# A fused linear-attention and max-out kernel on one core: the last scores of batch 0 moved between two projections, and four weight transposes moved into a wait

## The chip, the core and the metric

The kernel runs on one core of a Trainium2 chip. The core has TensorE (PE in the profile, with its weight loads as PEld), VectorE (DVE), ScalarE (ACT), GpSimd (POOL) and SyncE (SP), each with its own queue of instructions, worked off side by side and held together by semaphores; sixteen DMA engines move data between the chip's memory and the on-chip memory. Matmul results land in PSUM, which this kernel uses in banks of 128 x 512 numbers of 32 bits. The metric is the time of one execution on the device in microseconds (us), the median over runs.

## What is computed

Two stages, for 8 batches, 8 heads, 1024 positions and 64 features per head:

```python
k_proj = einsum('ks,bhsd->bhkd', E, k)          # 1024 positions -> 64
v_proj = einsum('ks,bhsd->bhkd', F, v)
scores = q @ k_proj.T / sqrt(64)
attn   = softmax(scores) @ v_proj               # 8 x 8 x 1024 x 64
x = attn.transpose(0, 2, 1, 3).reshape(8192, 512)
out = maximum(x @ w1, x @ w2) @ w_out           # 512 -> 1024 -> 512
```

## The kernel before

The kernel rewrites max(x w1, x w2) as relu(x (w1 - w2)) + x w2, so that out = relu(x wd) w_out + x m with wd = w1 - w2 and m = w2 w_out. For m it needs w2 transposed (`w2t_sb`); this takes 32 transposes of 128 x 128 on TensorE and copies out of PSUM on ScalarE. From batch 1 on, products are made with a seven-product (Strassen) scheme. Batch 0 is the start-up: its loads arrive piece by piece, and its order is written out by hand at L992 to L1041. The order of the program text is the order in every engine's queue, since scheduling is manual.

The steps that the change and the prediction speak of:

- `step_sc(t, g, j)` (L379): scores of head group g (four heads) and half j of the positions, 8 matmuls into a pair of "att" banks, then one exponential on ScalarE into `ex_sb`.
- `step_dn(t, g, j)` (L385): 8 matmuls with ones that sum the exponentials over the 64 projected positions, written over the scores' own bank pair, then a logarithm on ScalarE. `step_inv` (L428) turns it into the reciprocal (exponential of the negative) and sends a few rows by SyncE's queue to a table of checks.
- `step_kv(t, h0, h1, "v", ...)` (L185): projection of v for heads h0 to h1, 16 matmuls for two heads, then a cast to `vp_sb` by `copy` (DVE, or ACT for heads 4 to 8). `between` lets another step be issued between the two halves of its matmuls. v of batch 0 is loaded in four pieces of two heads.
- `step_at(t, g, j)` (L433): 16 value products (`values_into`, L365, through the helper at L355), into two "mm" banks or one att pair, then two multiplications by the reciprocal on DVE into `xt_sb`.
- `step_wd` (L543): w1 - w2 on DVE. `step_wd_rows` does the same in other pieces.
- `up_slots(t, j)` (L519): for half j the up blocks fb = 0 to 7 (called u0[fb] and u1[fb] after their half), each 4 matmuls of 128x512 into one mm bank, then a relu on ACT (DVE for fb = 3). The first two blocks of both halves are issued in two parts, `r1=2` and `r0=2`.
- `step_w2t(f0)` (L556): 8 transposes of w2 into one bank (an att bank with `att=True`), then one copy of 1024 on ACT.

PSUM is held in tiles by tag: four single banks mm0 to mm3 and two att pairs, used in turn. `mm_bank()` without a number takes the next of the list `turn`, which then moves on; with a number it takes that bank. An up block takes its bank by

```python
t["up", j, fb] = mm_bank(n=first_banks[j][fb] if r1 < NDC else fb % 2)
```

so the four blocks issued in two parts take their banks from `first_banks`, and later ones take bank 0 or 1. A bank can be written again when the last reader of its former tile is done. The order after L1041 is a list of slots: u0[0](r0=2), u0[1](r0=2), loads for batch 1, `step_w2t(256)`, u1[0](r0=2), u1[1](r0=2), subtractions, sums of x, u0[2], u0[3], then the Strassen products S1 and S2 (banks 2 and 3), the other transposes of w2, and so on.

Of the kernel before, what the change touches and what calls it, by code (L numbers as in the profile page):

```python
# [10 lines left out]
FP16 = mybir.dt.float16  # L11
# [8 lines left out]
def kernel(  # L20
# [12 lines left out]
    nc = tc.nc  # L33
# [29 lines left out]
    turn = [0, 1, 2, 3]  # L63

    def mm_bank(dtype=FP32, n=None):
        if n is None:
            n = turn.pop(0)
            turn.append(n)
        return ps.tile([128, 512 if dtype == FP32 else 1024], dtype, tag=f"mm{n}", name="mm_ps")

    def att_banks(dtype=FP32):
        return ps.tile(
            [128, 2, 512 if dtype == FP32 else 1024], dtype, tag="att", bufs=2, name="att_ps"
        )
# [4 lines left out]
    def big(n, dtype=FP16):  # L79
        return const.tile([128, 16384 // mybir.dt.size(dtype) // 2], dtype, tag=f"big{n}", name=f"big{n}")  # L80
# [45 lines left out]
    w2_sb = big(2).rearrange("p (r f) -> p r f", r=NDC)  # L126
    wo_sb = const.tile([128, NFB, DM], FP16, tag="wo", name="wo_sb")
    for g in range(2):
        for w_sb, w in ((w2_sb, moe_w2), (w1_sb, moe_w1)):
            nc.gpsimd.dma_start(  # L130
                out=w_sb.rearrange("p (g z) f -> p g z f", z=2)[:, g, :, 0:256],
                in_=w.rearrange("(g p z) f -> p g z f", p=128, z=2)[:, g, :, 0:256],
            )
    for w_sb, w, f0, f1 in (
# [3 lines left out]
        for z in range(2):  # L138
            nc.gpsimd.dma_start(
                out=w_sb.rearrange("p (g z) f -> p g z f", z=2)[:, :, z, f0:f1],  # L140
                in_=w.rearrange("(g p z) f -> p g z f", p=128, z=2)[:, :, z, f0:f1],
# [16 lines left out]
    ident16 = const.tile([128, 128], FP16)  # L158
# [26 lines left out]
    def step_kv(t, h0=0, h1=H, which="kv", att=False, dma=False, copy=nc.vector.tensor_copy, between=None):  # L185
        kv_ps = att_banks()[:, 0, :] if att else mm_bank(n=0 if dma else None)
        n = (h1 - h0) * D
        both = which == "v"
        nh = 2 if both else h1 - h0
        for h in range(0, h1 - h0, nh):  # L190
            if h and between is not None:
                between()
            for c in range(NC):
                for w in which:
                    i = "kv".index(w)
                    for r in range(2) if both else (i,):
                        nc.tensor.matmul(  # L197
                            out=kv_ps[r * KP : (r + 1) * KP, h * D : (h + nh) * D],
                            lhsT=eft[i][:, c, :],
                            rhs=t[w][:, h0 + h : h0 + h + nh, c, :],  # L200
                            start=(c == 0), stop=(c == NC - 1),
                        )
        zd = lambda ap: ap.rearrange("p (h d z) -> p h z d", d=D // 2, z=2)
        if "k" in which:
            eng = nc.vector.tensor_copy if which == "k" or dma else nc.scalar.copy
            kp = t["kp"][:, h0:h1]
            eng(out=kp[:, :, 0, :], in_=kv_ps[0:KP, 0:n].rearrange("p (h d) -> p h d", d=D))
        if both:
            copy(out=t["vp"][:, h0:h1], in_=zd(kv_ps[:, 0:n]))
        elif "v" in which:  # L210
            def finish_v():
                nc.vector.tensor_copy(out=t["vp"][KP:128, h0:h1], in_=zd(kv_ps[KP:128, 0:n]))
                if dma:
                    nc.vector.tensor_copy(out=kp[:, :, 1, :], in_=kp[:, :, 0, :])
                    step_kpt_dma(t)
                else:
                    step_vp(t, h0, h1)

            if att:
                return finish_v  # L220
            finish_v()


    def step_vp(t, h0=0, h1=H):
        fl = lambda ap: ap[:, h0:h1].rearrange("p h z d -> p (h z d)")
        nc.vector.tensor_copy(out=fl(t["vp"][0:KP]), in_=fl(t["vp"][KP:128]))
# [71 lines left out]
    def step_kpt_dma(t):  # L298
        nc.sync.dma_start_transpose(
            out=t["kpt"], in_=t["kp"].rearrange("p h r d -> p (h r d)")  # L300
        )
# [33 lines left out]
    def score(t, g, j, banks):  # L335
        for h in range(2):
            for o in range(2):
                for e in range(2):
                    head = 4 * g + 2 * h + e
                    z = D if t is tiles[0] else Z  # L340
                    for s in range(0, D, z):
                        pos = D * (o ^ e) + s
                        nc.tensor.matmul(  # L343
                            out=banks[e][pos : pos + z, h * W : (h + 1) * W],
                            lhsT=kpt_of(t, head, o)[:, s : s + z],
                            rhs=t["qt"][o * D : (o + 1) * D, head, j * W : (j + 1) * W],
                            start=True, stop=True,
                        )
        t["ex", g, j] = soft.tile([128, 2, HALF], FP16, tag="soft", name="ex_sb")
# [12 lines left out]
    def sums_into(t, g, j, dn_ps):  # L362
        tiles_into(lambda o: dn_ps[:, o, :], t["ex", g, j], lambda rows, hh: ones16[rows, 0:Z])
# [15 lines left out]
    def step_sc(t, g, j):  # L379
        sc_ps = att_banks()  # L380
        t["ps", g, j] = sc_ps
        score(t, g, j, [sc_ps[:, e, :] for e in range(2)])
        nc.scalar.activation(out=t["ex", g, j], in_=sc_ps, func=ACTF.Exp, scale=scale)

    def step_dn(t, g, j):  # L385
        dn_ps = t.pop(("ps", g, j))[:, :, 0:W]
        sums_into(t, g, j, dn_ps)
        ld = (ppool.tile([128, 2, W], FP32, tag="pd", bufs=4, name="ld_sb") if t is tiles[0]
              else soft.tile([128, 2, W], FP32, tag="soft", name="ld_sb"))
        t["ld", g, j] = ld  # L390
        nc.scalar.activation(out=t["ld", g, j], in_=dn_ps, func=ACTF.Ln)  # L391
# [4 lines left out]
    def check(inv):  # L396
        rows = checked[4 * n_checked[0] : 4 * n_checked[0] + 4, :]
        n_checked[0] += 1
        nc.sync.dma_start(
            out=rows, in_=inv.rearrange("(a z) o w -> a z (o w)", z=Z)[:, 0, :]  # L400
        )
# [26 lines left out]
    def step_inv(t, g, j):  # L428
        ld = t["ld", g, j]
        nc.scalar.activation(out=ld, in_=ld, func=ACTF.Exp, scale=-1.0)  # L430
        check(ld)
# [84 lines left out]
    w2t_sb = big(3).rearrange("p (f m) -> p f m", f=NFB)  # L516
# [32 lines left out]
    def step_wd_rows(f0):  # L549
        for z in range(2):  # L550
# [2 lines left out]
                out=rows(wd_sb), in0=rows(w1_sb), in1=rows(w2_sb), op=ALU.subtract  # L553
            )

    def step_w2t(f0, att=False, hold=False):  # L556
        ps_t = att_banks(FP16)[:, 0, :] if att else mm_bank(FP16)
        for f in range(2):
            for r in range(NDC):
                nc.tensor.transpose(  # L560
                    out=ps_t[:, (f * NDC + r) * 128 : (f * NDC + r + 1) * 128],
                    in_=w2_sb[:, r, f0 + f * 128 : f0 + (f + 1) * 128],
                    identity=ident16,
                )
        fb = f0 // 128

        def copy():
            nc.scalar.copy(
                out=w2t_sb[:, fb : fb + 2, :].rearrange("q f m -> q (f m)"), in_=ps_t
            )  # L570

        if hold:
            box["w2t"] = copy
        else:
            copy()
# [9 lines left out]
    CH = DM // 2  # L585
# [406 lines left out]
    t = tiles[0]  # L992
# [26 lines left out]
    warm(2)  # L1019
    step_sc(t, 1, 0)  # L1020
    step_kv(t, 0, 2, "v")
    step_kv(t, 2, 4, "v")
    step_dn(t, 1, 0)
    step_sc(t, 1, 1)
    step_at(t, 0, 0)
    step_at(t, 0, 1)
    step_inv(t, 1, 0)
    step_kv(t, 4, 8, "v", True, copy=nc.scalar.copy, between=lambda: step_dn(t, 1, 1))
    step_inv(t, 1, 1)
    att_banks()  # L1030
    for f0 in (0, 128):
        step_wd(f0, 0, 2, 128)
# [1 line left out]
    u0, u1 = [*up_slots(t, 0)], [*up_slots(t, 1)]  # L1034
    step_wd(0, 2, 4)
    step_at(t, 1, 1, True)
    first_banks = turn[0:2], turn[2:4]
    for i in range(2):
        for u in u0, u1:
            u[i](r1=2)  # L1040
    step_w2t(0, True)  # L1041


    load_all(tiles[1], 1, "k", k)
    wt = [lambda f0=f0: step_w2t(f0) for f0 in range(0, DF, 256)]
    wd = [lambda f0=f0: step_wd_rows(f0) for f0 in range(0, DF, 256)]
    f = lambda s, *a: lambda: s(tiles[0], *a)

    def loads(b, *names):
# [19 lines left out]
    slots = [  # L1069
        lambda: u0[0](r0=2), lambda: u0[1](r0=2), lambda: loads(1, "v", "q", "k"),  # L1070
        lambda: step_w2t(256, True),
        lambda: u1[0](r0=2), lambda: u1[1](r0=2), wd[1], lambda: sums_x(U[0, 1], range(4)),
        u0[2], u0[3], S1, S2, lambda: step_w2t(512, True), lambda: step_w2t(768, True, True), wd[2],
# [41 lines left out]
    t = tiles[1]  # L1115
    for n, x in enumerate((
# [4 lines left out]
        for name in x.split():  # L1121
# [6 lines left out]
            else:  # L1128
                g, j = int(name[2]), int(name[3])
# [14 lines left out]
    t = tiles[2]  # L1144
# [8 lines left out]
    for b in range(3, B):  # L1153
        t = tiles[b]
# [25 lines left out]
    for n, (b, o) in enumerate(units):  # L1180
# [14 lines left out]
        if n:  # L1195
            end = ("U", n - 1, 1, 6) if n > 1 else ("P", 0, 6, 1)
            m = 0 if n == last else 2
# [17 lines left out]
    for key, slot in slots:  # L1215
        r = slot()
        pending = [g for g in [r, *(f() for f in pending)] if g is not None]
        for s in steps.pop(key, ()):
            r = s()
# [5 lines left out]
    for reg in regs:  # L1225
# [4 lines left out]
        out=mm_bank()[0:1, 0:1], lhsT=ones16[:, 0:1], rhs=ones16[:, 0:1], start=True, stop=True  # L1230
# [166 lines left out]
```

## Time and profile before

| | us |
|---|---|
| median of three runs | 319.62 (319.59 to 319.87) |
| the profiled execution | 319.29 |
| its span, first to last instruction | 317.5 |

The span is the time that the profile shows; the 1.8 us around it are start and end of the execution. The mean granted TensorE clock of the execution is 0.999 of full speed.

How to read the rows. A row of the timeline has start and duration in us, the engine, the line of the kernel, the operation, the tile written and the tiles read, partitions x elements and type, and the count of instructions merged into the row; in brackets stands the idle time of the engine before it and what ended that. Matmuls overlap, so that a row of them can reach past the start of the next; the distance between starts is what they cost. A row of waits has the total, the number of waits and the longest. A row of a stretch has its limits, its length, then busy time and count for PE, PEld, DVE, ACT and POOL, the granted clock, the DMA share and GB/s.

### The profile page before, as it was taken

To read this page: it belongs to the slowest core of one execution; us is meant where nothing else is said; L and a number is where in the kernel's file an instruction comes from. 1 tells how busy PE (TensorE), PEld (TensorE's weight loads), DVE (VectorE), ACT (ScalarE), POOL (GpSimd) and SP (SyncE) were. 2 spreads that over 40 slices of the span, in tenths; PEclk is the share of its full clock that TensorE was granted. 3 is DMA by queue.
4 is the path that set the end of the run, shared out by engine and by line. 5 is a ranking of instruction groups with operands and counts; after the bars stand their busy time and mean duration, and the time that the engine had idled before them with its cause. 6 is when DMAs were issued, how large, how long until landed. Compare 5 with 4: busy or idle time off the path is not lost.

```text
span 317.5 us, 9309 instructions
## 1 busy us (share of the span) xinstructions
PE 311.7 (98%) x3902; PEld 254.9 (80%) x3902; DVE 244.9 (77%) x474; ACT 206.9 (65%) x375; POOL 39.7 (13%) x63
## 2 busy tenths in 40 slices
PE   7989999999999999999999999999999999999996
PEld 3656688788887888788887888788887888888885
DVE  3368997977969696996969696996969696969883
ACT  2477843767776777477776777476776777765541
POOL 8269002011000400003000300003000000000000
PEclk9999999999999999999999999999999999999999
DMA  8999999999978799997999699987998431313134
GB/s 190 206 201 199 207 206 202 208 166 165 185 144 193 135 195 245 235 190 118 226 242 243 124 199 246 218 164 124 224 222 204 90 101 36 103 34 102 35 102 136
DMA packets 76685, 53.72 MB, mean 169 GB/s; under 512 B 29664, under 2 KB 76128, under 8 KB 76640
## 3 DMA queue, kind: packets, MB, share of 16 engines
q0 software_dynamic: 30688, 28.05, 56.2%
q1 hardware_dynamic: 45664, 24.85, 31.5%
q8 instruction: 31, 0.51, 0.7%
q10 hardware_dynamic: 288, 0.20, 0.2%
q14 instruction: 14, 0.11, 0.1%
HBM read 57.15 MB, written 16.78 MB: 233 GB/s over the span
## 4 chain that ended last, share of the span: by engine, by line
PE 92%; DMA 5%; POOL 1%; ACT 1%; issue 0%; DVE 0%; POOLq 0%
PE mm_ps L874 47%; PE mm_ps L766 28%; DMA v_sb<-in_v_dram 4%; PE att_ps L355 3%; PE mm_ps L528 3%; PE mm_ps L197 3%; PE mm_ps L343 2%; PE att_ps L239 1%; PE att_ps L644 1%; PE mm_ps L644 1%; DMA out_dram<-o_sb 1%; PE mm_ps L313 1%; PE att_ps L560 1%; POOL k_sb L108 0%; POOL q_sb L108 0%; ACT ld_sb L391 0%
## 5 line engine op out<-in xcount | busy, mean ns | idle before, releaser
L736 ACT COPY p_sb<-mm_ps 128x512 f32<-128x512 f32 x180 | 102.4, 592 | 47.3 <-PE mm_ps L766 27.2
L874 PEld LDWEIGHTS <-big 128*128 128x128 f16 x768 | 73.5, 98 | 11.8 <-issue 3.6
L874 PE MATMUL mm_ps<-T_sb,big 128*128 128x256 f16 x576 | 76.9, 273 | 0.0
L781 DVE TENSOR_TENSOR gt_sb<-mm_ps,p_sb 128x512 f16<-128x512 f32 x58 | 39.9, 688 | 42.8 <-PE mm_ps L766 41.4
L766 PE MATMUL mm_ps<-big,big 128*128 128x256 f16 x348 | 52.2, 273 | 0.0
L766 PEld LDWEIGHTS <-big 128*128 128x128 f16 x464 | 45.4, 98 | 5.9 <-DVE big L607 0.2
L874 PE MATMUL mm_ps<-wo_sb,gt_sb 128*128 128x256 f16 x256 | 42.6, 273 | 0.0
L874 PEld LDWEIGHTS <-gt_sb 128*128 128x128 f16 x376 | 35.7, 98 | 6.7 <-issue 2.7
L472 ACT ACTIVATE ex_sb<-mm_ps 128x512 f16<-128x512 f32 x50 | 27.2, 596 | 18.0 <-PE mm_ps L343 12.3
L766 PEld LDWEIGHTS <-wd_sb 128*128 128x128 f16 x348 | 34.1, 98 | 4.4
L766 PE MATMUL mm_ps<-xt_sb,wd_sb 128*128 128x256 f16 x232 | 33.8, 273 | 0.0
L502 DVE TENSOR_TENSOR xt_sb<-att_ps,ld_sb 128x1024 f16<-128x1024 f32 x26 | 31.7, 1218 | 0.2
L874 PE MATMUL mm_ps<-m_sb,xt_sb 128*128 128x256 f16 x128 | 24.5, 273 | 0.0
L905 DVE TENSOR_TENSOR o_sb<-mm_ps,p_sb 128x512 f32<-128x512 f32 x32 | 21.8, 683 | 2.8 <-ACT p_sb L934 2.0
L784 DVE TENSOR_SCALAR gt_sb<-gt_sb 128x512 f16<-128x512 f16 (+1 forms) x62 | 21.8, 351 | 2.1
L305 POOL COPY junk<-qt_sb 1x1 f16<-1x1 f16 x6 | 1.4, 238 | 174.1 <-DMA qt_sb<-q_sb 174.1
L719 DVE TENSOR_TENSOR big<-gt_sb 128x1024 f16<-128x1024 f16 x32 | 21.8, 682 | 0.0
L874 PE MATMUL mm_ps<-wo_sb,big 128*128 128x256 f16 x128 | 21.5, 273 | 0.0
L843 ACT ACTIVATE gt_sb<-mm_ps 128x512 f16<-128x512 f32 x29 | 17.4, 600 | 5.9 <-PE mm_ps L766 5.9
L874 PE MATMUL mm_ps<-T_sb,gt_sb 128*128 128x256 f16 x120 | 20.3, 273 | 0.0
L781 DVE TENSOR_TENSOR gt_sb<-p_sb 128x512 f16<-128x512 f32 x29 | 19.8, 682 | 0.6 <-ACT p_sb L736 0.6
L874 PEld LDWEIGHTS <-xt_sb 128*128 128x128 f16 x188 | 18.3, 98 | 2.3 <-issue 0.2
(123 smaller groups left out, 432.9 us busy)
## 6 DMA issues: line engine op xcount, KB each, us to landing
out_dram<-o_sb SPq DMA_DIRECT2D x62, 256.0 KB
k_sb<-in_k_dram POOLq DMA_DIRECT2D x7, 1024.0 KB, 10.2
v_sb<-in_v_dram POOLq DMA_DIRECT2D x7, 1024.0 KB, 17.0
q_sb<-in_q_dram POOLq DMA_DIRECT2D x5, 1024.0 KB, 23.5
q_sb<-in_q_dram POOLq DMA_DIRECT2D x6, 512.0 KB, 16.1
big<-in_moe_w_dram POOLq DMA_DIRECT2D x12, 128.0 KB, 6.5
v_sb<-in_v_dram POOLq DMA_DIRECT2D x4, 256.0 KB, 13.4
wo_sb<-in_moe_w_out_dram POOLq DMA_DIRECT2D x1, 1024.0 KB, 10.3
```

What stands on the lines that cost most here:

```text
L197: nc.tensor.matmul(out=kv_ps[r * KP : (r + 1) * KP, h * D : (h + nh) * D], lhsT=eft[i][:, c, :], rhs=t[w][:, h0 + h : h0 + h + nh, c, :], ...
L355: nc.tensor.matmul(out=dst(r ^ (hh % 2))[hh * Z : (hh + 1) * Z, :], lhsT=weights(rows, hh), rhs=ex[rows, hh % 2, hh // 2 * W : (hh // 2 + ...
L472: nc.scalar.activation(out=t["ex", g, j][:, e, :], in_=banks[e], func=ACTF.Exp, scale=scale)
L502: nc.vector.tensor_tensor(out=x_out(t, g, j).rearrange("q z o n -> q o z n"), in0=at_ps.rearrange("q o (z n) -> q o z n", z=2), in1=ld[:, ...
L719: nc.vector.tensor_tensor(out=S(i), in0=S(0) if x is None else x, in1=y(), op=op)
L736: copy(out=x, in_=bank)
L766: nc.tensor.matmul(out=bank[:, m * W : (m + 1) * W], lhsT=w_[:, n_, (2 * d + m) * 128 : (2 * d + m + 1) * 128], rhs=a[:, n_, :], start=(n ...
L781: nc.vector.tensor_tensor(out=c_blk(j, c), in0=two(x), in1=two(y), op=ALU.add)
L784: nc.vector.tensor_scalar_max(ap, ap, 0.0)
L843: nc.scalar.activation(out=out, in_=in_, func=ACTF.Relu)
L874: nc.tensor.matmul(out=bank[i][:, 0:CH] if two_banks else bank[:, i * CH : (i + 1) * CH], lhsT=a(c)[:, i * 128 : (i + 1) * 128], rhs=w_(c) ...
L905: nc.vector.tensor_tensor(out=o_sb, in0=two(x), in1=two(y), op=ALU.add)
```

## The change

In the hand-written order of batch 0, sc(1,1) goes ahead of the second v projection; dn(1,1) goes ahead of the projection of heads 4 to 8, which is issued in one piece; four of the first eight transposes of w2 (the row blocks r = 0 and 1 of the first two column blocks) go behind that projection into a single mm bank, with their copy behind the second reciprocal; the other four stay where all eight were. The bank used is the first of `turn`, which is not moved on, and the banks of the first up blocks are shifted by one, so that the last of them, u1[1], gets the bank of the four transposes.

```diff
+    def step_w2t_half(g, ps_t):
+        for f in range(2):
+            for z in range(2):
+                r = 2 * g + z
+                nc.tensor.transpose(
+                    out=ps_t[:, (f * 2 + z) * 128 : (f * 2 + z + 1) * 128],
+                    in_=w2_sb[:, r, f * 128 : (f + 1) * 128], identity=ident16,
+                )
+        return lambda: nc.scalar.copy(
+            out=w2t_sb[:, 0:2, g * CH : (g + 1) * CH],
+            in_=ps_t[:, 0 : 2 * CH].rearrange("q (f m) -> q f m", f=2),
+        )
+
     step_sc(t, 1, 0)
     step_kv(t, 0, 2, "v")
+    step_sc(t, 1, 1)
     step_kv(t, 2, 4, "v")
     step_dn(t, 1, 0)
-    step_sc(t, 1, 1)
     step_at(t, 0, 0)
     step_at(t, 0, 1)
     step_inv(t, 1, 0)
-    step_kv(t, 4, 8, "v", True, copy=nc.scalar.copy, between=lambda: step_dn(t, 1, 1))
+    step_dn(t, 1, 1)
+    step_kv(t, 4, 8, "v", True, copy=nc.scalar.copy)
+    w2t_copy = step_w2t_half(0, mm_bank(FP16, turn[0]))
     step_inv(t, 1, 1)
+    w2t_copy()
     att_banks()
...
-    first_banks = turn[0:2], turn[2:4]
+    first_banks = turn[1:3], (turn[3], turn[0])
     for i in range(2):
         for u in u0, u1:
             u[i](r1=2)
-    step_w2t(0, True)
+    step_w2t_half(1, att_banks(FP16)[:, 0, :])()
```

## The prediction

> **What bounds the kernel now.** I read the page first, then the list of what TensorE (PE) waited for, then the timeline from 17 to 30 us, where the edited steps lie.
>
> ```profile
> PE 311.7 (98%) x3902; PEld 254.9 (80%) x3902; DVE 244.9 (77%) x474; ACT 206.9 (65%) x375; POOL 39.7 (13%) x63
> ...
> PE 92%; DMA 5%; POOL 1%; ACT 1%; issue 0%; DVE 0%; POOLq 0%
> ```
>
> ```profile
> ...
> PE mm_ps L1229 <- DMA out_dram<-o_sb: 1.2, 1, 1.2
> PE att_ps L355 <- ACT vp_sb L209: 0.5, 1, 0.5
> PE mm_ps L197 <- DMA v_sb<-in_v_dram: 0.4, 1, 0.4
> PE att_ps L355 <- ACT ex_sb L383: 0.2, 1, 0.2
> ```
>
> The page's two rows are busy time by engine and the chain that ended last by engine. The four rows of PE's waits (total, times, longest) are all of its waits from 17 us to the end. The L1229 wait is the very last instruction. So from 22.6 us to about 313 us PE never stands still, and whatever PE gains or loses before about 30 us moves the end by the same amount: there is no later wait that could give back a gain or swallow a loss. The three short waits, 1.1 us together, are what the change can go for.
>
> ```profile
> 17.68 0.64 PE L197 MATMUL mm_ps<-v_sb,eft 128*64 128x128 f16 x16
> 18.77 0.64 PE L197 MATMUL mm_ps<-v_sb,eft 128*64 128x128 f16 x16 [0.45 <-DMA v_sb<-in_v_dram]
> 19.34 0.30 PE L355 MATMUL att_ps<-ex_sb,ones 64*32 64x256 f16 x8
> 19.57 0.41 PE L343 MATMUL att_ps<-qt_sb,kpt_sb 64*64 64x256 f16 x8
> 19.91 0.63 PE L355 MATMUL mm_ps<-ex_sb,vp_sb 64*32 64x256 f16 x32
> 20.47 0.64 PE L197 MATMUL att_ps<-v_sb,eft 128*64 128x128 f16 x16
> 21.27 0.30 PE L355 MATMUL att_ps<-ex_sb,ones 64*32 64x256 f16 x8 [0.16 <-ACT ex_sb L383]
> 21.50 0.64 PE L197 MATMUL att_ps<-v_sb,eft 128*64 128x128 f16 x16
> 22.61 0.63 PE L355 MATMUL att_ps<-ex_sb,vp_sb 64*32 64x256 f16 x32 [0.47 <-ACT vp_sb L209]
> 23.21 1.90 PE L528 MATMUL mm_ps<-xt_sb,wd_sb 128*128 128x512 f16 x8
> 24.95 0.61 PE L560 MATMUL att_ps<-ident,big 128*128 128x128 f16 x8
> 25.39 1.03 PE L528 MATMUL mm_ps<-xt_sb,wd_sb 128*128 128x512 f16 x4
> 26.26 0.61 PE L560 MATMUL att_ps<-ident,big 128*128 128x128 f16 x8
> 26.70 2.75 PE L528 MATMUL mm_ps<-xt_sb,wd_sb 128*128 128x512 f16 x12
> 29.29 0.49 PE L766 MATMUL mm_ps<-xt_sb,wd_sb 128*128 128x256 f16 x3
> ```
>
> These are start and duration. A row's price on PE is the distance to the next start, since matmuls overlap: 16 of a v projection 0.57 (18.77 to 19.34), 8 sums 0.23, 8 scores 0.34, 32 value products 0.56, 8 transposes 0.44 (so four 0.22), four 128x512 matmuls 0.87. The twelve at 26.70 are the second halves of up blocks u1[0] and u1[1], then u0[2] and u0[3]; 2.59/12 = 0.216 each puts u0[2] at 26.70 + 4 x 0.216 = 27.56. That moment is my yardstick.
>
> **The change part by part.**
>
> *The last scores, sc(1,1), ahead of the second v projection.* They run from 18.25 (17.68 + 0.57) to 18.59, inside the DMA wait that ends at 18.77, and cost nothing there; with that cover gone they would cost 0.34. What they leave behind is not worth 0.34 either, for the next value products wait for a cast:
>
> ```profile
> 19.45 0.29 DVE L209 CAST vp_sb<-mm_ps 128x128 f16<-128x128 f32 x1 [0.79 <-PE mm_ps L197]
> 20.47 2.48 DVE L446 TENSOR_TENSOR xt_sb<-mm_ps,ld_sb 128x512 f16<-128x512 f32 x4 [0.73 <-PE mm_ps L355]
> 22.87 0.48 DVE L544 TENSOR_TENSOR wd_sb<-big,big 128x256 f16<-128x256 f16 x2
> ...
> 24.80 1.28 DVE L446 TENSOR_TENSOR xt_sb<-att_ps,ld_sb 128x512 f16<-128x512 f32 x2
> ```
>
> ```profile
> 17.81 1.02 ACT L383 ACTIVATE ex_sb<-att_ps 128x1024 f16<-128x1024 f32 x1 [0.55 <-PE att_ps L343]
> 19.71 0.60 ACT L391 ACTIVATE ld_sb<-att_ps 128x512 f32<-128x512 f32 x1 [0.88 <-PE att_ps L355]
> 20.20 1.02 ACT L383 ACTIVATE ex_sb<-att_ps 128x1024 f16<-128x1024 f32 x1
> ...
> 22.18 0.37 ACT L209 CAST vp_sb<-att_ps 128x256 f16<-128x256 f32 x1
> 22.45 0.63 ACT L430 ACTIVATE ld_sb<-ld_sb 128x512 f32<-128x512 f32 x1
> ```
>
> The vector engine's (DVE's) cast ends at 19.74; a hop to PE is 0.06 (ACT's cast ends at 22.55, PE goes on at 22.61). So at(0,0) starts at 19.80 in place of 19.91: gain 0.11, with bounds 0 and 0.34. On ScalarE (ACT) the exponential of sc(1,1) moves from 20.20 to about 18.8, into idle time, and the logarithm at 19.71 stays.
>
> *dn(1,1) ahead of the last v projection, which is no longer split.* Value products 19.80 to 20.36, dn(1,1) to 20.59 without its 0.16 wait (the exponential is done at 19.8), first half of the projection to 21.16. The second half needs the last piece of v:
>
> ```profile
> L108 POOL DMA_DIRECT2D v_sb<-in_v_dram x2: 738/746/755, 6.3 to 7.0; - x2
> DMA to landing us min/median/max: 13.7/14.0/14.3
> ```
>
> These are the last two v issues; the later one, at 7.0, lands at 7.0 + 14.3 = 21.3. So a stall of 0.18 comes in the middle, the second half starts at 21.34 where it started at 21.50, and the rest follows 0.16 earlier: ACT's cast 22.02 to 22.39, at(1,0) at 22.45. No DMA issue changes its place in SyncE's or GpSimd's queue.
>
> *Four transposes in the wait for that cast.* PE is free from 21.91 to 22.45 and they take 0.22: free. Their bank, number 0, is left by DVE's first product at about 21. If the wait were gone they would cost the 0.22 that the shorter block at 24.95 saves. Their copy follows the reciprocal on ACT, 22.83 to about 23.4, before u1[1] first writes the bank at about 24.4.
>
> *Up to here.* DVE's products run back to back from 20.47, so they too come only 0.11 earlier, and the up blocks, which wait for the subtraction at 22.87, start at 23.10. Eight matmuls to 24.84, four transposes to 25.06, u0[0] and u0[1] to 25.93. The eight transposes of the next block need the bank that DVE leaves at 26.08 - 0.11 = 25.97, so 26.03 to 26.47, and u1[0], u1[1] to 27.34. That is a gain of 0.22, and it would be the whole story were the banks as before.
>
> *The banks of the up blocks.* After 24 turns the list stands at 0, 1, 2, 3. Before, u0[0], u0[1], u1[0], u1[1] got 0, 1, 2, 3; now they get 1, 2, 3, 0. The next block, u0[2], has bank fb % 2 = 0 fixed in the code. It therefore used to wait for the relu of u0[0], the oldest; it now waits for the relu of u1[1], the block computed immediately before it. In the changed kernel's order this shows: u0[2]'s first matmul waits for ACT and the three blocks after it need no further wait.
>
> ```profile
> 25.59 1.01 ACT L568 COPY big<-att_ps 128x1024 f16<-128x1024 f16 x1 [2.51 <-PE att_ps L560]
> 26.50 1.09 ACT L537 ACTIVATE gt_sb<-mm_ps 128x512 f16<-128x512 f32 x2
> 27.47 1.03 ACT L568 COPY big<-att_ps 128x1024 f16<-128x1024 f16 x1
> 28.36 1.62 ACT L537 ACTIVATE gt_sb<-mm_ps 128x512 f16<-128x512 f32 x3
> ```
>
> ACT's order is copy, two relus (u0[0], u0[1]), copy, two relus (u1[0], u1[1]). From start to start a big copy takes 0.90, a relu 0.49 ((27.47 - 26.50)/2). Before, u1[1]'s relu began at 28.85, but only the second Strassen product at 29.7 needed it. Now: the half copy is not in the trace; it lies between the cast of 256 (0.37) and the copy of 1024 (1.01), and I take the relu's 0.49, of 512 elements from the same memory. It starts 0.42 after its transposes (24.95 to 25.59 is 0.64, less 0.22), at 25.26; relus at 25.75 and 26.24; the big copy at 26.73 (its transposes are ready at 26.03 + 0.64 = 26.67); u1[0]'s relu at 27.62, u1[1]'s at 28.11, done at 28.71 with 0.60; u0[2] at 28.76.
>
> PE has nothing else to do from 27.34 to 28.76: behind u0[2] in its queue stand u0[3] and all later products, and ACT's relu of u0[2] and DVE's of u0[3] wait for these. The stall is 1.42 and the sum 1.42 - 0.22 = **+1.20 us**. Bounds: no gain at the value products gives +1.31; DVE as early as PE's own work allows (up blocks at 23.01) +1.11; a half copy as dear as the big one, +1.61; free, +1.15 (the relus then follow PE).
>
> The Trainium skill, "PSUM — Partial Sum Buffer", section "Engine vs sequencer instructions", says that ScalarE's queue is strictly first in, first out. By that rule u1[1]'s relu can't pass the big copy, and the sum stays at +1.20. Were it wrong, the relu could start with u1[1]'s end, and the sum would be that of the third case below.
>
> **The rivals.** (a) *The bank does not bind*, and only the gain stays: 319.62 - 0.22 = 319.4. u1[1]'s relu would have to end by 27.28, and ACT's rows put it 1.4 later; for it speaks only that ACT may take the half copies faster than any row here, or the bank order may be other than I read. This is the other side: not slower.
>
> (b) *The clock falls in the stall.* The first matmuls of the kernel ran at half the later speed, and PE's clock stayed full over a shorter wait:
>
> ```profile
> 1.47 3.60 PE L153 MATMUL mm_ps<-ones 128*128 128x512 f16 x8 [1.47 <-DVE ones L146]
> ```
>
> ```profile
> 21.50:22.61 1.11, 0.64 (x25) 0.48 (x17) 1.11 (x3) 1.11 (x4) 1.07 (x2) 1.00 1.44 192
> ```
>
> Eight 128x512 matmuls took 3.60 there against 8 x 0.216 = 1.73 now. If the stall brought that state back for u0[2] and u0[3], eight such matmuls, 1.8 us would come on top: 322.6. Against it: in the second row PE was busy for 0.64 of 1.11 us and the last-but-two number, the clock, stayed 1.00. The Trainium skill, "TensorE: Matmul & The Clock Gate", section "What's actually happening", has the clock halve after an idle window of about 3.4 us; a stall of 1.42 is shorter, and no run here shows that window.
>
> (c) *ACT frees the bank without the big copy ahead of it*: relu of u1[1] behind that of u1[0] from 27.1, done near 28.2, +0.6 to +0.7: 320.3. Against it stands that the rows at 26.50, 27.47 and 28.36 run in program order.
>
> (d) *The loss is absorbed later*, 319.6 to 320.2. The list of waits leaves no place for it.
>
> **How the numbers follow.** The profiled execution took 319.29 us (span 317.5 and 1.8 around it); with +1.20 it would be 320.49. The median of the runs is 0.33 higher, so the forecast for the median is 319.62 + 1.20 = 320.8. Chances: forecast 0.80, (a) 0.07, (b) 0.04, (c) 0.06, (d) 0.03. Less than 0.2%, or 0.64 us, can't be told from no change. The forecast is slower by 0.38%, and its bounds of +1.11 to +1.61 all are; (a) is mostly within, (c) on the edge, (d) within. So slower 0.83, the same 0.13, faster 0.04. The range from 320.2 to 321.5 takes in the bounds, the scatter of 0.3 among the runs before, and (c).
>
> **What would show it.** In the changed profile PE's waits should list a new one, L528 on ACT's relu, of about 1.4 us, near 27.3; it should end with the second relu after the big copy. sc(1,1) should lie at about 18.3, at(0,0) at 19.8, the up blocks at 23.1, u0[2] near 28.8, and everything after it 1.2 us later with no other new wait. Of PE's old waits for the exponential and for v's second piece the first should be gone and the second shortened. I am wrong if u0[2] follows u1[1] directly, or if a wait after 30 us shrinks by what this one costs.

## The result, and the profile after

The changed kernel takes 320.89 us (median of 18 runs, 320.53 to 323.14) against 319.71 us (18 runs, 319.36 to 320.48) beside it: 1.18 us more, ratio 1.0038 with a 95% interval of 1.0029 to 1.0046. It is slower, by the amount that was forecast. Its profiled execution took 320.90 us with a span of 319.0. The ratios, here and below, leave out slow executions, of which there is one, 1126.80 us among the nine of experiment e4 (its median keeps it), and they need not equal the quotient of the two medians.

PE's waits in the changed kernel (total, times, longest):

```profile
PE mm_ps L153 <- DVE ones L146: 1.5, 1, 1.5
PE mm_ps L528 <- ACT gt_sb L537: 1.2, 1, 1.2
PE mm_ps L1245 <- DMA out_dram<-o_sb: 1.2, 1, 1.2
PE att_ps L197 <- DMA v_sb<-in_v_dram: 0.2, 1, 0.2
PE att_ps L343 <- DVE qt_sb L318: 0.2, 1, 0.2
PE mm_ps L197 <- DMA v_sb<-in_v_dram: 0.2, 1, 0.2
```

The three waits that the change went for are smaller or gone: the one for ACT's cast of v (0.5) and the one for the exponential (0.2) are no longer listed, the one for v's second piece fell from 0.4 to 0.2. In their place stands a wait of an up block (L528) for a relu (L537), larger than all three together, and v's last piece is now waited for. PE's timeline around it, start and duration first:

```profile
17.59 0.41 PE L343 MATMUL att_ps<-qt_sb,kpt_sb 64*64 64x256 f16 x8
...
18.50 0.41 PE L343 MATMUL att_ps<-qt_sb,kpt_sb 64*64 64x256 f16 x8
19.07 0.64 PE L197 MATMUL mm_ps<-v_sb,eft 128*64 128x128 f16 x16 [0.16 <-DMA v_sb<-in_v_dram]
...
21.64 0.64 PE L197 MATMUL att_ps<-v_sb,eft 128*64 128x128 f16 x16 [0.24 <-DMA v_sb<-in_v_dram]
22.29 0.40 PE L560 MATMUL mm_ps<-ident,big 128*128 128x128 f16 x4
22.73 0.63 PE L355 MATMUL att_ps<-ex_sb,vp_sb 64*32 64x256 f16 x32
23.38 1.90 PE L528 MATMUL mm_ps<-xt_sb,wd_sb 128*128 128x512 f16 x8
25.11 0.39 PE L560 MATMUL att_ps<-ident,big 128*128 128x128 f16 x4
25.34 1.03 PE L528 MATMUL mm_ps<-xt_sb,wd_sb 128*128 128x512 f16 x4
26.40 0.61 PE L573 MATMUL att_ps<-ident,big 128*128 128x128 f16 x8
26.84 1.03 PE L528 MATMUL mm_ps<-xt_sb,wd_sb 128*128 128x512 f16 x4
29.09 1.89 PE L528 MATMUL mm_ps<-xt_sb,wd_sb 128*128 128x512 f16 x8 [1.23 <-ACT gt_sb L537]
30.82 1.04 PE L779 MATMUL mm_ps<-xt_sb,wd_sb 128*128 128x256 f16 x8
```

In the kernel before, twelve matmuls stood in one row from 26.70: u1[0], u1[1], u0[2], u0[3]. Now the row is broken after four. Counted from start to start, u1's four cost 4 x 0.216 = 0.86 from 26.84, so PE stood from 27.70 to 29.09, 1.39 us. (The row's 1.23 counts from the modelled end of the last matmul.) The chain of waits of the same execution says what it waited on, link by link:

```profile
25.28 0.24 PE att_ps L560 x4
25.52 0.02 issue
25.54 0.58 ACT big L564
26.12 0.99 ACT gt_sb L537 x2
27.11 0.94 ACT big L581
28.05 1.00 ACT gt_sb L537 x2
29.05 0.04 issue
29.09 1.89 PE mm_ps L528 x8
```

Half copy, two relus, big copy, two relus, and 0.04 later u0[2]: for 3.5 us the time of the kernel is set by ACT.

The two profiled executions did not start alike: v's first projection, ahead of which nothing was changed, began at 17.68 before and at 17.93 here. The second, which follows the landing of its piece of v in both, began at 18.77 and at 19.07. So I compare by the distance from that start to u0[2]: 27.56 - 18.77 = 8.79 before, 29.09 - 19.07 = 10.02 here, +1.23. The rest of the 1.53 by which u0[2] is later here is the later start. What becomes of it afterwards is in the chain's last links, of the kernel before and of the changed one:

```profile
313.59 1.98 DMA out_dram<-o_sb
```

```profile
315.12 1.98 DMA out_dram<-o_sb
```

The last store starts 1.53 later, exactly as u0[2] does: over 285 us nothing was given back and nothing was added.

### The profile page after: what moved, and what is told of

It reads as the page before. It is cut to its first block, busy times and chain, and to the rows that moved or that the text cites. A ratio compares the mean times of both kernels' runs of the same rounds, so it can differ in the third digit from the quotient of the medians.

```text
span 319.0 us, 9309 instructions
## 1 busy us (share of the span) xinstructions
PE 312.7 (98%) x3902; PEld 254.9 (80%) x3902; DVE 244.7 (77%) x474; ACT 207.2 (65%) x376; POOL 39.9 (13%) x63
## 4 chain that ended last, share of the span: by engine, by line
PE 91%; DMA 5%; POOL 2%; ACT 1%; issue 0%; DVE 0%; POOLq 0%
PE mm_ps L887 47%; PE mm_ps L779 28%; DMA v_sb<-in_v_dram 5%; PE att_ps L355 3%; PE mm_ps L197 3%; PE mm_ps L528 3%; PE mm_ps L343 2%; PE att_ps L239 1%; PE att_ps L657 1%; PE mm_ps L657 1%; POOL v_sb L108 1%; ACT gt_sb L537 1%; DMA out_dram<-o_sb 1%; PE mm_ps L313 1%; POOL k_sb L108 0%; POOL q_sb L108 0%
## 6 DMA issues: line engine op xcount, KB each, us to landing
k_sb<-in_k_dram POOLq DMA_DIRECT2D x7, 1024.0 KB, 10.2
```

## The experiments

Two theories. The *bank theory* is that of the prediction: u0[2]'s fixed bank 0 went to u1[1], so it waits for the youngest relu in place of the oldest. The *order theory*: the moves and the split copy delay ACT or PE by themselves, whatever the banks. Each kernel's time stands against runs of the kernel before beside it on the same chip.

| kernel | median, us | before beside it | ratio (95%) | second v projection to u0[2], against 8.79 |
|---|---|---|---|---|
| the change | 320.89 | 319.71 | 1.0038 (1.0029 to 1.0046) | +1.23 |
| e1_banks_turned | 319.61 | 319.69 | 0.9995 (0.9986 to 1.0004) | -0.15 |
| e2_banks_alone | 321.67 | 319.69 | 1.0057 (1.0042 to 1.0071) | +1.99 |
| e3_order_alone | 319.68 | 319.69 | 1.0007 (0.9990 to 1.0024) | -0.13 |
| e4_copy_held | 320.37 | 319.69 | 1.0025 (1.0015 to 1.0035) | +0.76 |
| e5_all_eight | 320.29 | 319.82 | 1.0013 (1.0004 to 1.0021) | +0.37 |
| e6_eight_old_order | 320.32 | 319.82 | 1.0010 (0.9989 to 1.0030) | +0.46 |
| e7_u1_first | 319.63 | 319.84 | 0.9992 (0.9973 to 1.0011) | -0.25 |
| e8_banks_turned_again | 319.60 | 319.84 | 0.9995 (0.9979 to 1.0012) | -0.16 |

The medians are of 18 runs for the change, 4 for e2, 9 for e4 and 11 or 12 for the others. The last column is from one profile of each kernel; where u0[2] has no row of its own, it is the start of u1's row plus 0.86, and in e6 the second projection is taken 0.57 ahead of the sums at 19.72. In e5 the scores ahead of the second projection ended only after its piece of v had landed (issued at 5.5, landed 13.6 later, at 19.1; the projection began at 19.38), so that its +0.37 leaves out some 0.2 us.

### e1_banks_turned: the banks put right, all else as changed

```diff
+    turn.insert(0, turn.pop())
     step_kv(t, 0, 2, "v")
```

> The changed kernel with the list of banks turned by one before the v projections, so that the four transposes and u1[1] share bank 3 and u0[0], u0[1], u1[0] get 0, 1, 2 as in the kernel before. Bank theory (u0[2] stalls because its fixed bank 0 was given to u1[1]): no wait of u0[2] on ACT, u0[2] about 0.2 us earlier than before, 319.4 to 319.5 us against 319.7. Order theory (the new order and the split copies themselves delay ACT or PE, whatever the banks): still about 320.9.

PE's timeline of this kernel:

```profile
25.51 1.03 PE L528 MATMUL mm_ps<-xt_sb,wd_sb 128*128 128x512 f16 x4
26.57 0.61 PE L573 MATMUL att_ps<-ident,big 128*128 128x128 f16 x8
27.02 2.75 PE L528 MATMUL mm_ps<-xt_sb,wd_sb 128*128 128x512 f16 x12
```

The twelve matmuls are one row again, and the time is that of the kernel before. The v projections and value products have their banks turned by one as well, but all moves of the change are in this kernel, so the order theory falls. The gain came out at 0.15 us in the trace, not 0.2, and the runs cannot tell it from nothing. The rows say why: PE was done with u0's four at 25.51 + 0.86 = 26.37 and began the second transposes at 26.57, for these write the bank that DVE's last product reads:

```profile
25.14 1.28 DVE L446 TENSOR_TENSOR xt_sb<-att_ps,ld_sb 128x512 f16<-128x512 f32 x2
```

It ends at 26.42. DVE's chain, not PE, sets this place; e5, where these transposes get another bank, bears that out.

### e2_banks_alone: only the banks shifted, the kernel before otherwise

```diff
-    first_banks = turn[0:2], turn[2:4]
+    first_banks = turn[1:3], (turn[3], turn[0])
```

> The kernel before with the four up blocks' banks shifted as in the change (1, 2, 3, 0) and nothing else changed. Bank theory: u0[2] waits for u1[1]'s relu, which in the kernel before began at 28.85 and so ends at 29.45; u0[2] at 29.5 in place of 27.56, so a stall of 1.9 us, more than in the changed kernel: 321.6. Order theory: no change, 319.7.

PE's timeline:

```profile
26.97 1.03 PE L528 MATMUL mm_ps<-xt_sb,wd_sb 128*128 128x512 f16 x4
29.81 1.89 PE L528 MATMUL mm_ps<-xt_sb,wd_sb 128*128 128x512 f16 x8 [1.81 <-ACT gt_sb L537]
31.53 1.04 PE L766 MATMUL mm_ps<-xt_sb,wd_sb 128*128 128x256 f16 x8
```

This one line alone costs +1.98 us in the medians, +1.99 in the trace; +1.94 was expected. PE stands from 26.97 + 0.86 = 27.83 to 29.81, 1.98 us. It is dearer than the whole change: with the eight transposes in one block ACT's first copy starts later (25.86 - 19.03 = 6.83 after the second v projection, against 25.54 - 19.07 = 6.47 in the change) and is longer (1.01 against 0.58), so u1[1]'s relu ends later.

### e3_order_alone: the two moves without the transposes and the banks

```diff
+    step_sc(t, 1, 1)
     step_kv(t, 2, 4, "v")
     step_dn(t, 1, 0)
-    step_sc(t, 1, 1)
...
-    step_kv(t, 4, 8, "v", True, copy=nc.scalar.copy, between=lambda: step_dn(t, 1, 1))
+    step_dn(t, 1, 1)
+    step_kv(t, 4, 8, "v", True, copy=nc.scalar.copy)
```

> The kernel before with the two moves alone: sc(1,1) ahead of the second v projection, dn(1,1) ahead of the last one, which is no longer split; the eight transposes and the banks as before. Bank theory: no stall; the up blocks come 0.1 us earlier, 319.6. Order theory: slower by most of the 1.2 us, 320.5 to 320.9.

No difference in the runs; 0.13 us ahead in the trace, 0.1 expected. Moving four transposes into the wait (e1) adds only 0.02 to that, one trace against one: of the 0.22 that PE saves there it loses 26.57 - 26.37 = 0.20 waiting for DVE.

### e4_copy_held: the big copy behind the relus

```diff
-        lambda: step_w2t(256, True),
-        lambda: u1[0](r0=2), lambda: u1[1](r0=2), wd[1], lambda: sums_x(U[0, 1], range(4)),
+        lambda: step_w2t(256, True, True),
+        lambda: u1[0](r0=2), lambda: u1[1](r0=2), lambda: box.pop("w2t")(), wd[1], lambda: sums_x(U[0, 1], range(4)),
```

> The changed kernel with ACT's big copy of the second transposes held until behind u1[1]'s relu; banks as in the change. Bank theory with the length of the stall set by ACT's queue: u1[1]'s relu begins as soon as its matmuls end, near 27.6 on the scale of the profile before, the stall of u0[2] shrinks from 1.4 to about 0.85 us, 320.3. If the stall's length has nothing to do with ACT's queue: 320.9, as the changed kernel.

ACT's timeline, then PE's:

```profile
25.97 1.09 ACT L537 ACTIVATE gt_sb<-mm_ps 128x512 f16<-128x512 f32 x2
27.42 1.09 ACT L537 ACTIVATE gt_sb<-mm_ps 128x512 f16<-128x512 f32 x2 [0.36 <-PE mm_ps L528]
28.39 1.02 ACT L581 COPY big<-att_ps 128x1024 f16<-128x1024 f16 x1
```

```profile
26.34 0.61 PE L573 MATMUL att_ps<-ident,big 128*128 128x128 f16 x8
26.79 1.03 PE L528 MATMUL mm_ps<-xt_sb,wd_sb 128*128 128x512 f16 x4
28.56 1.89 PE L528 MATMUL mm_ps<-xt_sb,wd_sb 128*128 128x512 f16 x8 [0.74 <-ACT gt_sb L537]
```

ACT now waits 0.36 for u1[0] instead of being busy with the copy, and the stall is 28.56 - 26.79 - 0.86 = 0.91. The loss fell to +0.68 in the medians. So 0.48 of the 1.39 came from the copy ahead of the relus in ACT's queue; the 0.91 that is left lies between u1's last matmul and the end of its relu. That ScalarE's queue is strictly first in, first out, as the Trainium skill says ("PSUM — Partial Sum Buffer", "Engine vs sequencer instructions"), fits: from 27.06 to 27.42 ACT stood idle for u1[0]'s relu, while the copy behind it was ready, for its transposes had ended at 26.34 + 0.61 = 26.95.

### e5_all_eight and e6_eight_old_order: all eight transposes in the wait

In e5 the e1 kernel, in e6 the kernel before with the banks turned; in both the block of eight goes where the change put four. The edit of e5:

```diff
...
     step_kv(t, 4, 8, "v", True, copy=nc.scalar.copy)
-    w2t_copy = step_w2t_half(0, mm_bank(FP16, turn[0]))
+    step_w2t(0, hold=True, bank=turn[0])
     step_inv(t, 1, 1)
-    w2t_copy()
+    box.pop("w2t")()
...
-    step_w2t_half(1, att_banks(FP16)[:, 0, :])()
```

> The kernel with the banks turned (e1_banks_turned), with all eight transposes of the first block in the wait for the last v cast and none behind the up blocks. That kernel moved u0[2] only 0.14 us ahead of the kernel before, counted from the start of v's second projection, because its second transposes waited for the att bank that DVE's last product leaves. Theory: that bank, not PE, took the rest of the gain; here the second transposes get the other att bank, free 1.3 us earlier, so the wait goes, PE saves the 0.22 of four more transposes, and u0[2] lies 0.5 to 0.55 us ahead of the kernel before: 319.1 to 319.3. Rival: DVE's chain or the landing of w2's second columns holds u1[0] anyway, and the time stays at 319.6.

> The kernel before with its own order of scores and sums, banks turned, and all eight transposes in the wait for the last v cast. Theory: the 0.44 us of the eight transposes goes from PE's busy stretch into its wait, and neither the scores' nor the sums' new place is needed for that: u0[2] 0.4 us ahead, 319.3. Rival: the gain needs the earlier order, since DVE's chain starts no earlier: 319.6 to 319.7.

Both theories missed, and neither rival names what happened. e5 is 0.47 us slower than the kernel before by the medians, with an interval clear of no change. e6 is 0.50 slower by the medians, but its interval takes in no change; its trace is 0.46 behind. PE's timeline of e5, then its chain of waits:

```profile
22.30 0.28 PE L573 MATMUL mm_ps<-ident,big 128*128 128x128 f16 x2
23.63 0.51 PE L573 MATMUL mm_ps<-ident,big 128*128 128x128 f16 x6 [1.05 <-DMA big<-in_moe_w_dram]
24.07 0.63 PE L355 MATMUL att_ps<-ex_sb,vp_sb 64*32 64x256 f16 x32
24.63 2.76 PE L528 MATMUL mm_ps<-xt_sb,wd_sb 128*128 128x512 f16 x12
```

```profile
13.52 10.06 DMA big<-in_moe_w_dram
23.58 0.05 issue
23.63 0.51 PE mm_ps L573 x6
```

The second half of w2's rows is issued at 13.52 and lands at 23.58, after the wait is over. PE stood 1.05 us, the value products behind the transposes with it; in e6 the same wait is 0.75. The rest of the theory shows in the same rows: no transposes stand behind the first up blocks, and twelve up matmuls run in one row. The second transposes, in the other att bank, follow these at 27.23 without a pause (24.63 + 12 x 0.216 = 27.22), though DVE's last product ends only at 27.44. So only four transposes can go in this wait because only their rows have landed. The profile before had it: there the same load, issued at 13.01, took 10.2 and so landed at 23.2, and the wait ended at 22.61.

### e7_u1_first and e8_banks_turned_again

e8 is e1 once more; e7 changes the order in it:

```diff
-        lambda: step_w2t(256, True),
-        lambda: u1[0](r0=2), lambda: u1[1](r0=2), wd[1], lambda: sums_x(U[0, 1], range(4)),
+        lambda: u1[0](r0=2), lambda: u1[1](r0=2), lambda: step_w2t(256, True), wd[1], lambda: sums_x(U[0, 1], range(4)),
```

> The kernel with the banks turned (e1_banks_turned), with u1[0] and u1[1] (second parts) issued ahead of the second eight transposes. Theory: in e1 the transposes of the second block began 0.15 us after DVE's last product freed their att bank, with PE idle for 0.19 us; u1[0] needs the same product's result, but only that, and the transposes then follow without a wait. u0[2] should lie 0.2 to 0.25 us ahead of the kernel before, counted from the start of v's second projection, against 0.14 in e1; the time 319.4 to 319.6. Rival: the hop from DVE is paid by u1[0] in the same way, and nothing is gained over e1.

> The same kernel as e1_banks_turned, beside e7_u1_first on the same chip. Theory: 0.1 to 0.2 us ahead of the kernel before, which the interval may or may not tell from nothing; e7_u1_first 0.1 us ahead of it. Rival: no gain over the kernel before.

PE's timeline of e7:

```profile
25.64 1.99 PE L528 MATMUL mm_ps<-xt_sb,wd_sb 128*128 128x512 f16 x8
27.47 0.61 PE L573 MATMUL att_ps<-ident,big 128*128 128x128 f16 x8
27.91 1.89 PE L528 MATMUL mm_ps<-xt_sb,wd_sb 128*128 128x512 f16 x8
```

In the trace e7 is where it was expected, 0.25 us ahead of the kernel before and 0.1 ahead of e1. The rival is right in part: u1[0] pays for the step from DVE too, since the eight matmuls from 25.64 take 1.83 us and not 1.73. In the runs neither can be told from the kernel before, nor from each other: a version that surely beats it was not found. e1, e7 and e8 do beat the changed kernel, by 1.3 to 1.4 us when each is taken against the kernel before beside it.

## Why the prediction was right

- *The scores in the DMA wait.* They were to start 0.91 after the scores before them; 18.50 - 17.59 = 0.91. They cost nothing.
- *The value products.* A gain of 0.11 was forecast. DVE's first product started 20.47 - 18.77 = 1.70 after the second projection before and 20.64 - 19.07 = 1.57 now, a gain of 0.13. That all of at(0,0) waits for the second cast was not quite right: heads 0 and 1 need only the first, so that its first products run ahead and PE pauses among them.

```profile
20.64 2.48 DVE L446 TENSOR_TENSOR xt_sb<-mm_ps,ld_sb 128x512 f16<-128x512 f32 x4 [0.60 <-ACT ld_sb L391]
...
24.97 1.28 DVE L446 TENSOR_TENSOR xt_sb<-att_ps,ld_sb 128x512 f16<-128x512 f32 x2
```

- *The unsplit projection.* A stall of 0.18 for v's last piece was forecast. Counted in the same way, from start to start, 21.64 - 20.76 - 0.57 = 0.31 came. The difference is in the first half, which began 20.76 - 19.07 = 1.69 after the second projection, where 20.59 - 18.77 = 1.82 was forecast, because the value products had started early and the sums behind them ended early. The second half began when forecast, 2.57 after the second projection in both, for the landing sets it. In e1, e3, e4 and e8 the wait is listed too, with 0.20 to 0.27 (0.24 here); in e5 and e7, where the start-up ran later, it is not.
- *The four transposes.* They were free, as forecast, but with luck: the prediction asked only for PE and a bank, not for the landing of the rows that they read. Here that load was issued at 7.63 and took 14.6, so it landed at 22.2, and the weight load of the first transpose waited 0.18 for it. By their price of 0.22 the four were through at 22.29 + 0.22 = 22.51, and the value products began at 22.73. A landing more than 0.22 later would have held these up, as a later one does in e5.
- *The gain as far as u1.* Forecast 0.22, measured (26.70 - 18.77) - (26.84 - 19.07) = 0.16. The term that was mis-sized is the step from DVE's last product to the second transposes: 0.06 taken, 26.40 - (24.97 + 1.28) = 0.15 measured, and 0.15 again in e1. A plain matmul that waits for the same product in e7 follows it by 0.06 (25.27 + 1.28 = 26.55, start at 26.61). Ahead of the transposes the trace has an extra semaphore instruction in the queue of the weight loads, at 26.3 and 0.051 long, which may be part of the difference; no run tests it.
- *ACT's queue.* Its rows now:

```profile
25.54 0.58 ACT L564 COPY big<-att_ps 128x512 f16<-128x512 f16 x1 [1.85 <-PE att_ps L560]
26.02 1.09 ACT L537 ACTIVATE gt_sb<-mm_ps 128x512 f16<-128x512 f32 x2
27.04 1.01 ACT L581 COPY big<-att_ps 128x1024 f16<-128x1024 f16 x1
27.95 1.09 ACT L537 ACTIVATE gt_sb<-mm_ps 128x512 f16<-128x512 f32 x2
```

From start to start the half copy took 0.48 (0.49 taken), the big copy 0.91 (0.90). From the half copy's start to u0[2] it is 29.09 - 25.54 = 3.55, against 28.76 - 25.26 = 3.50. Of the 0.05 more, 0.04 lies at the two relus, 1.02 from 26.02 to the big copy at 27.04, against 0.98 taken. The copy began 0.64 after its transposes (26.40), the time that the prediction takes for it to be ready, so the late step from DVE may show here once more.
- *The stall* was to be 1.42 and was 1.39; the sum +1.20, and +1.23 in the trace, +1.18 in the medians.
- *No later wait gives it back:* the shift of the last store equals that of u0[2].

Of the rivals, (a), that the bank does not bind, fell with e1 and e2. (c) was built in e4 and cost 0.76 in the trace, where 0.6 to 0.7 was estimated. (d) fell with the last store. (b), a lower clock, can't be answered from the clock in the row of a stretch, on which the prediction leaned. That number, the last but two, is the clock that was granted, and it reads 1.00 also over the kernel's first matmuls, which ran at half the later speed, 3.60 us for eight; in the kernel before:

```profile
0.00:5.00 5.00, 3.53 (x9) 1.04 (x9) 1.74 (x21) 1.28 (x1) 3.87 (x11) 1.00 0.58 155
```

What answers it is the speed behind the stall. The eight matmuls of u0[2] and u0[3] took from 29.09 to 30.82 in the changed kernel, 1.73 us, and from 29.81 to 31.53 in e2, 1.72 us behind a stall of 1.98, the longest before u0[2] in these runs. Eight took 8 x 0.216 = 1.73 in the kernel before, so the half speed did not come back. The idle window of about 3.4 us after which the clock halves, in the Trainium skill ("TensorE: Matmul & The Clock Gate", "What's actually happening"), agrees as far as this goes; no stall here was that long.

## What to carry to other kernels

When a bank is lent to another step, follow who gets it next, to the end of the rotation: a bank that passes from the oldest reader to the youngest turns a wait of nothing into the whole queue of the engine that reads it, and one shifted assignment cost more than all the waits that the change could win. That wait could be read off the code before anything ran: `fb % 2` is fixed, and the list beside it was shifted. And a wait of 0.5 us is only worth the work whose inputs have landed and whose successors are not held by another engine: here four transposes could go in and four could not, and DVE's chain kept most of what the four saved.

## What the runs showed of the hardware

The start-up scatters by more than the gains sought: v's first projection, ahead of which all these kernels have the same program, began between 17.68 and 18.52 in their profiles, and the second between 18.77 and 19.39. Gains of 0.1 to 0.25 us that single traces show could not be told from nothing by the medians of 11 or 12 runs. And loads of equal size took longer to land the earlier they were issued in the start-up: in the profile before, four of 128 KB issued at 7.66, 10.51, 13.01 and 15.55 took 14.3, 12.1, 10.2 and 8.4 us, where the median of the twelve loads of that size is 6.5.
